# Attention's q products as 64-row halves of the array in token pairs, and inverse roots on VectorE

## The chip, the core and the metric

The kernel runs on one core of a Trainium2 chip. The metric is device microseconds of one execution; the median of three runs of the kernel before is 1817.77 us (1817.72 to 1819.34). TensorE (PE) multiplies, with its weight loads (PEld) recorded apart; VectorE (DVE), ScalarE (ACT) and GpSimd (POOL) work element by element; SyncE (SP) issues most of the DMAs. Each engine works through its own list in order.

## The reference

```python
kv = np.einsum('bhsd,bhse->bhde', k, v)          # batch 8, heads 8, seq 576, head_dim 64
out = np.einsum('bhsd,bhde->bhse', q, kv)
rms = np.sqrt(np.mean(out * out, axis=-1, keepdims=True) + 1e-06)
attn = (out / rms * g_norm).astype(np.float32)
x = attn.transpose(0, 2, 1, 3).reshape(4608, 512)
# then twice, with its own weights: x = (act(x @ w_gate) * (x @ w_val)) @ w_out
# act: sigmoid the first time, silu the second; w_gate, w_val 512 x 1536, w_out 1536 x 512
```

All is float32. The attention is linear: for each head a 64 x 64 product of k and v, then q times it, then a norm over the head's 64 values.

## The kernel before, in words

The two feed-forward layers hold nearly all of the arithmetic. They are four phases of matmuls (`PH`); phase 0, the first 400 us or so, runs `gv_plain` (lines 638 to 646) and `part_plain` (806), the later ones `gv_win` (709) and `out_win` (841). Attention is not a stage of its own. A short prologue does batch 0's k-v product and the first four token tiles; everything else of it stands in a queue of steps, `att`, and is dropped between the feed-forward matmuls of phase 0 by `tick`, early enough for the block of 512 tokens that needs it (`AHEAD`).

A token tile is 128 tokens of a batch with all 8 heads. There are 36: nine per pair of batches, and the fifth of each nine (i == R) holds the last 64 tokens of both batches; we call it a rest tile. For each tile `tok_q` and `tok_a` bring q transposed into `qT` (128 partitions: two heads of 64, by four head pairs, by 128 tokens), `tok_b` multiplies it with k-v (207 or 209) and squares the result on ACT (212), `tok_r` sums the squares (DVE, 216) and takes the inverse root, `tok_n` scales the product (239) into `xn`, and `tok_c` transposes it and sends it to memory. `STAGES` sets by how many tiles each step follows the first.

In `tok_b` the k-v product of a head pair is a block-diagonal 128 x 128 matrix in `kvz`, with zeros off the diagonal that POOL writes once. So a tile is four matmuls over all 128 rows of the array, 128 tokens as weights and 128 moving columns. Its result fills one PSUM bank of the pool `ps_g`, which has four and serves the gate and value products (`gv`) too. Each float32 matmul shows in the trace as two weight loads and two matmul records. A rest tile writes its two batches to the two 64-column halves of the array.

The inverse root is ACT's table function in the first four tiles, after which one Newton step follows on DVE; in the other 32 tiles it is `pow` on POOL (222) with the Newton step on POOL (230 to 233). ACT loads the table of `Abs_reciprocal_sqrt` at the start (84), and another when the first sigmoid comes (645).

Weights of later phases are prepared by `stage`: a list of small steps that begins with the loads of raw weights (`l0`, `l1`, `l2`), then `nop` steps that give the DMA time, and then `o1` and so on, of which `o1` (375) is ACT's and waits for the raw weights to land. PE, DVE and SP are ordered by a scheduler in this stretch; ACT and POOL go as the code is written.

Of the kernel before, what the change touches and what calls it, by code (L numbers as in the profile page):

```python
# [9 lines left out]
F32 = mybir.dt.float32  # L10
F32R = mybir.dt.float32r
U32 = mybir.dt.uint32
AF = mybir.ActivationFunctionType
ALU = mybir.AluOpType
AX = mybir.AxisListType
# [5 lines left out]
def attention_two_ffn(ctx: ExitStack, tc: tile.TileContext, q, k, v, g_norm, weights, out):  # L21
# [8 lines left out]
    nc = tc.nc  # L30
    B, H, S, D = q.shape
# [3 lines left out]
    P = 128  # L35
    NB = 512
    NBLK = NT // NB
    TPB = NB // P
    KD = DM // P
    NP = H // 2  # L40
    R = 4
    KB = 1024
    SM = R * P
    SR = S - SM
    TP = 2 * S // P
# [3 lines left out]
    sm = ctx.enter_context(tc.tile_pool(name="sm", bufs=4))  # L49
    dr = ctx.enter_context(tc.tile_pool(name="dr", bufs=1, space=DRAM))  # L50
    ps_o = ctx.enter_context(tc.tile_pool(name="ps_o", bufs=4, space=PSUM))
    ps_g = ctx.enter_context(tc.tile_pool(name="ps_g", bufs=4, space=PSUM))
# [4 lines left out]
    at = at_ctx.enter_context(tc.tile_pool(name="at", bufs=1, side="right"))  # L57
# [15 lines left out]
    early = tc.manual_schedule(engines={ET.Activation, ET.Pool})  # L73
    early.__enter__()
    ident = at.tile([P, P], F32, name="ident")
    kvz = [at.tile([P, NP, 2, D], F32, name=f"kvz{i}") for i in range(2)]
    gcol = at.tile([P, 1], F32, name="gcol")
    mhalf = at.tile([P, H], F32, name="mhalf")
    grow = at.tile([P, D], F32, name="grow")
    make_identity(nc, ident)  # L80
    for t in kvz:
        nc.gpsimd.memset(t, 0.0)
    nc.vector.memset(mhalf, -0.5)
    nc.scalar.activation(sm.tile([P, H], F32, tag="y", name="y"), mhalf, AF.Abs_reciprocal_sqrt)


    MANUAL = (0, 4)
    TA = 11
    SQ = 32
    QB, XT = 4, 5 * TPB  # L90
    kvt, qt, kvps, kvbd, qT, xn, xd = {}, {}, {}, {}, {}, {}, {}
    xr = {}
    for j in range(NBLK):
        t = dr.tile([DM, NB], F32, name=f"xd{j}")
# [39 lines left out]
    def run_of(b, nm, r, hs=slice(0, H)):  # L134

        if (b, nm, r) not in kvt:
            tag, n = ("ta", TA) if b == 0 else (nm + "s", 2)
            kvt[b, nm, r] = at.tile([P, H, D], F32, tag=tag, bufs=n, name=f"{nm}s")
# [20 lines left out]
                nc.tensor.matmul(kvps[b][e * D:(e + 1) * D, hp, :D], lt, rt, start=(r == hp == 0), stop=(r == R and hp == NP - 1), skip_group_check=True)  # L159

    def kv_mask(b):
        ps, z = kvps.pop(b), kvz[b % 2]
        for e in range(2):
            es = slice(e * D, (e + 1) * D)
            if b < 1:
                nc.vector.tensor_copy(out=z[es, :, e], in_=ps[es, :, :D])
            else:
                nc.scalar.activation(z[es, :, e], ps[es, :, :D], AF.Copy)
        kvbd[b] = z.rearrange("p a e d -> p a (e d)")

    def tok_q(tau):
        bp, i = divmod(tau, TP)
        b = 2 * bp + (i > R)
        if b >= QB and i != R:
            n = P // SQ
            src = kvt[b, "q"][:, :, (i if i < R else i - R - 1) * n:][:, :, :n]
            qT[tau] = at.tile([P, NP, P], F32, tag="ta", bufs=TA, name="qT")
            nc.vector.transpose(qT[tau].rearrange("p a (j c) -> p a j c", c=SQ), src)
# [3 lines left out]
    def tok_a(tau):  # L182
# [4 lines left out]
        for hp in range(NP):  # L187
# [5 lines left out]
            nc.tensor.transpose(ps[:, hp, :], src, ident)  # L193
        qT[tau] = at.tile([P, NP, P], F32, tag="ta", bufs=TA, name="qT")
        nc.scalar.activation(qT[tau], ps, AF.Copy)

    sqt, ost = {}, {}

    def tok_b(tau):
        bp, i = divmod(tau, TP)  # L200
        t = qT.pop(tau)
        ps = ps_g.tile([P, NP, P], F32, tag="g", name="ops")
        for hp in range(NP):
            if i == R:
                for e in range(2):
                    es = slice(e * SR, (e + 1) * SR)
                    nc.tensor.matmul(ps[es, hp, :], t[:, hp, es], kvbd[2 * bp + e][:, hp, :], start=True, stop=True)
            else:
                nc.tensor.matmul(ps[:, hp, :], t[:, hp, :], kvbd[2 * bp + (i > R)][:, hp, :], start=True, stop=True)  # L209
        ost[tau] = ps.rearrange("p a (b d) -> p (a b) d", d=D)  # L210
        sqt[tau] = at.tile([P, H, D], F32, tag="ta", bufs=TA, name="sq")
        nc.scalar.activation(sqt[tau], ost[tau], AF.Square)

    def tok_r(tau):
        a = sm.tile([P, H], F32, tag="a", name="a")
        nc.vector.tensor_reduce(a, sqt.pop(tau), axis=AX.X, op=ALU.add)
        (nc.vector if tau < TPB else nc.gpsimd).tensor_scalar(a, a, 1.0 / D, 1e-6, op0=ALU.mult, op1=ALU.add)
        y = sm.tile([P, H], F32, tag="y", name="y")
        if tau < TPB:
            nc.scalar.activation(y, a, AF.Abs_reciprocal_sqrt)  # L220
        else:
            nc.gpsimd.tensor_tensor(out=y, in0=a, in1=mhalf, op=ALU.pow)
        u = sm.tile([P, H], F32, tag="u", name="u")
        if tau < TPB:
            nc.vector.scalar_tensor_tensor(out=u, in0=y, scalar=-0.5, in1=y, op0=ALU.mult, op1=ALU.mult)
            nc.vector.tensor_tensor(out=u, in0=u, in1=a, op=ALU.mult)
            nc.vector.scalar_tensor_tensor(out=y, in0=u, scalar=1.5, in1=y, op0=ALU.add, op1=ALU.mult)
            sqt[tau] = y
            return
        nc.gpsimd.tensor_tensor(out=u, in0=y, in1=y, op=ALU.mult)  # L230
        nc.gpsimd.tensor_tensor(out=u, in0=u, in1=a, op=ALU.mult)
        nc.gpsimd.tensor_scalar(u, u, -0.5, 1.5, op0=ALU.mult, op1=ALU.add)
        nc.gpsimd.tensor_tensor(out=y, in0=y, in1=u, op=ALU.mult)
        sqt[tau] = y

    def tok_n(tau):
        y = sqt.pop(tau)
        xn[tau] = at.tile([P, H, D], F32, tag="ta", bufs=TA, name="xn")
        nc.vector.tensor_tensor(out=xn[tau], in0=ost.pop(tau), in1=y.unsqueeze(2).to_broadcast([P, H, D]), op=ALU.mult)
        if tau >= XT:  # L240
            nc.gpsimd.tensor_tensor(out=xn[tau], in0=xn[tau], in1=grow.unsqueeze(1).to_broadcast([P, H, D]), op=ALU.mult)

    def tok_c(tau):
        if tau >= XT:
# [30 lines left out]
    def attention_steps():  # L275

        st = []
        nt = B * S // P
        STAGES = ((0, tok_q), (1, tok_a), (3, tok_b), (3, tok_r), (4, tok_n), (5, tok_c))

        def run(t0, t1):
            for t in range(t0, t1 + 5):
                bp, i = divmod(t, TP)
                b = 2 * bp + (i >= R)
                z = i - R * (b % 2)
                on = t < t1 and b + 1 < B
                kv = list(kv_of(b + 1)) if on and z == 2 + b % 2 else []
                qs = [lambda b=b, a=a: load_q(b + 1, a) for a in range(NP)] if kv and b + 1 >= QB else []
                if t < t1 and i == 1:
                    st.append((t, lambda bp=bp: load_qr(bp)))  # L290
                for lag, f in STAGES:
                    if t0 <= t - lag < t1:
                        st.append((t - lag, lambda t=t - lag, f=f: f(t)))
                    if lag == 3:
                        st.extend((t, f) for f in kv[:1])
                        del kv[:1]
                        if not kv:
                            st.extend((t, f) for f in qs[:1])
                            del qs[:1]
                    elif not kv:  # L300
                        st.extend((t, f) for f in qs[:1])
                        del qs[:1]
                st.extend((t, f) for f in qs)
                if on and z == 3 + b % 2:
                    if b + 1 < QB:
                        st.append((t, lambda b=b: load_q(b + 1)))
                    if b + 2 < B:
                        st.append((t, lambda b=b: load_kv(b + 2)))

        st.append((TPB, lambda: load_kv(2)))  # L310
        run(TPB, nt)
        return st


    PROLOGUE = "w9 K q0 q1 a0 a1 q2 q3 w1 kv b0 a2 lq qr r0 b1 a3 r1 n0 w6 b2 r2 c0 n1 b3 r3 c1 n2 w3 c2 n3 c3 k6 w6"


    PH = [(0, 0, 6, False), (0, 6, 6, True), (1, 0, 6, True), (1, 6, 6, True)]
# [104 lines left out]
    def stage(f, m):  # L423
# [7 lines left out]
        e = m % 2  # L431
        paired = phase_of[f, m][0] in WOUT
        d = wd[f, m] = dr.tile([P, E + (0 if paired and not e else E if paired else 2 * DM)], F32, name=f"wd{f}_{m}")
        z = {}
# [16 lines left out]
        l0, o0, s0 = rounded(f, m - e, e, buf)  # L451
        l1, o1, s1 = rounded(f, m - e + 1, e, buf)
        l2, o2, s2 = rounded(f, m, 2, buf)

        def new(k):
            z[k] = buf("s")
# [6 lines left out]
        q0 = lambda i: lambda: s0["u"][:, i * Q:(i + 1) * Q]  # L463
        q1 = lambda i: lambda: s1["u"][:, i * Q:(i + 1) * Q]
        S = lambda k, i: lambda: z[k][:, i * Q:(i + 1) * Q]
        th = [l0, l1, nop, nop] + o0 + o1
        th += [lambda: (new(0), sm_(0, 0, q1(0), q1(1), ALU.add)())]
        th += [sm_(0, 1, S(0, 0), q0(0), ALU.subtract)]
        th += [lambda: (new(1), sm_(1, 0, q0(0), q1(0), ALU.subtract)())]
# [14 lines left out]
        ]  # L484
        if paired:
            return th + (stage_pair(f, m, buf, store, fl, hi, lo) if e else [])
        return th + [l2, nop, nop, nop] + o2 + [
            lambda: hi(fl(s2, 0, 2), s2["u"]),
            lambda: lo(fl(s2, 2, 4), s2["u"], fl(s2, 0, 2)),
            nop,  # L490
# [132 lines left out]
    ht, ops, part, pd = {}, {}, {}, {}  # L623
# [522 lines left out]
    for ph, (f, m0, n, win) in enumerate(PH):  # L1146
# [4 lines left out]
        for at_, (j, ms) in enumerate(visits):  # L1151
# [6 lines left out]
            for i in ms:  # L1158
# [42 lines left out]
                if tail and tail[0] + 1 < len(PH) and tail[1] == NBLK - 1 and PH[tail[0]][3]:  # L1201
                    z = tail[2] - PH[tail[0]][1]
# [53 lines left out]
```

## Time and profile before

| what | value |
|---|---|
| median of the runs | 1817.77 us |
| profiled execution, its own time | 1813.71 us |
| its span, first to last instruction | 1811.9 us |
| PE busy | 1776.1 us, 98% |
| DVE, ACT, POOL busy | 1055.2, 661.7, 684.5 us |
| granted TensorE clock, mean | 0.996 |

The profiled execution took 1.8 us more than its span, before the first or after the last instruction. The sums below are made against this execution, and a difference found there is carried over to the median, which is 4.06 us higher. A busy PE is one with a matmul under way; the mean duration of a matmul record is from its start to its end in the array, and several overlap, so the pace is read from how far the starts lie apart, or from the chain of waits, which gives each piece the time until the next one began.

### The profile page before, as it was taken

How to read it: one execution, taken by the hardware profiler on the slowest of the kernel's cores; microseconds unless marked ns; L12 is line 12 of the kernel's file. 1: busy time of each engine (PE TensorE's matmuls, PEld its weight loads, DVE VectorE, ACT ScalarE, POOL GpSimd, SP SyncE). 2: the span in 40 equal slices, each digit the busy share in tenths (PEclk: the TensorE clock that was granted, in tenths of full speed). 3: DMA queues.
4: the chain of work that ended last, by engine and by line, in shares of the span. 5: the costliest groups of instructions: out<-in, count | busy, mean ns of one | idle time of the engine just before them, and what ended most of it. 6: DMA issues, size and time to landing. Idle time of an engine off the chain costs nothing.

```text
span 1811.9 us, 31885 instructions
## 1 busy us (share of the span) xinstructions
PE 1776.1 (98%) x12298; PEld 1625.4 (90%) x12298; DVE 1055.2 (58%) x1754; ACT 661.7 (37%) x1349; POOL 684.5 (38%) x748
## 2 busy tenths in 40 slices
PE   5899999999999999999999999999999999999999
PEld 4688887888889999999999999999999999999998
DVE  5866466554335666666666565555553555555555
ACT  3654233333233333333333443334342333333332
POOL 1654355431012442442433443344441344444444
PEclk8999999999999999999999999999999999999999
DMA  9968875557236542434339755555567634343432
GB/s 265 271 176 222 236 195 154 139 148 242 93 116 250 181 136 91 146 99 135 127 130 402 282 182 176 190 186 187 192 231 286 232 129 129 129 129 129 129 129 71
DMA packets 274824, 320.38 MB, mean 177 GB/s; under 512 B 95856, under 2 KB 193392, under 8 KB 271984
## 3 DMA queue, kind: packets, MB, share of 16 engines
q1 hardware_dynamic: 259504, 305.24, 52.1%
q10 hardware_dynamic: 15168, 13.11, 2.5%
q8 instruction: 96, 1.57, 0.4%
q14 instruction: 56, 0.46, 0.1%
HBM read 191.14 MB, written 127.14 MB: 176 GB/s over the span
## 4 chain that ended last, share of the span: by engine, by line
PE 93%; DMA 2%; DVE 2%; SPq 1%; ACT 1%; issue 1%; POOL 0%; DVEq 0%; ACTq 0%
PE gv L709 44%; PE o L820 16%; PE gv L638 15%; PE o L806 8%; PE o L841 7%; PE ops L209 1%; DMA raw<-in_moe_w_out_dram 1%; PE kvps L159 1%; DMA xl<-xd 0%; DMA vm<-in_v_dram 0%; PE xTp L256 0%; PE qTp L193 0%; DMA raw<-in_moe_w_gate_dram 0%; ACT u L375 0%; SPq L126 0%
## 5 line engine op out<-in xcount | busy, mean ns | idle before, releaser
L709 PE MATMUL gv<-x,wgv 128*128 128x256 f32 x4536 | 549.3, 282 | 0.0
L709 PEld LDWEIGHTS gv<-x,wgv 128*128 128x128 f32 x4536 | 545.5, 189 | 2.8 <-DVE v L329 0.2
L638 PE MATMUL gv<-x,wgv 128*128 128x512 f32 x1296 | 314.3, 394 | 5.3 <-ACT sg L645 3.7
L638 PEld LDWEIGHTS gv<-x,wgv 128*128 128x128 f32 x1296 | 240.3, 188 | 56.7 <-ACT sg L645 4.6
L709 PEld LDWEIGHTS gv<-arena,wgv 128*128 128x128 f32 x2268 | 273.7, 190 | 2.8 <-DVE v L329 0.4
L709 PE MATMUL gv<-arena,wgv 128*128 128x256 f32 x2268 | 274.6, 282 | 0.1
L329 DVE TENSOR_TENSOR u<-u,gv 128x512 f32<-128x512 f32 x162 | 110.9, 684 | 260.5 <-PE gv L709 256.0
L697 POOL TENSOR_TENSOR h<-v,h 128x512 fp32r<-128x512 f32 x54 | 75.0, 1388 | 243.7 <-ACT h L693 243.4
L806 PE MATMUL o<-h,wo 128*128 128x512 f32 x648 | 164.2, 397 | 0.0
L682 ACT ACTIVATE w<-v 128x256 f32<-128x256 f32 x81 | 34.0, 420 | 313.8 <-DVE v L329 306.5
L806 PEld LDWEIGHTS o<-h,wo 128*128 128x128 f32 x648 | 120.0, 188 | 27.1 <-issue 0.3
L697 POOL TENSOR_TENSOR h<-w,h 128x512 fp32r<-128x512 f32 x54 | 70.7, 1310 | 140.6 <-ACT h L693 137.7
L820 PE MATMUL o<-arena,h 128*128 128x512 f32 x432 | 103.6, 395 | 0.0
L820 PE MATMUL o<-h,arena 128*128 128x512 f32 x432 | 103.3, 394 | 0.0
L646 DVE TENSOR_TENSOR sg<-sg,gv 128x512 f32<-128x512 f32 x54 | 36.9, 684 | 109.1 <-PE gv L638 108.9
L820 PEld LDWEIGHTS o<-arena,h 128*128 128x128 f32 x432 | 79.9, 188 | 17.9
L820 PEld LDWEIGHTS o<-h,arena 128*128 128x128 f32 x432 | 80.1, 188 | 17.5
L753 POOL TENSOR_TENSOR he<-w,he 128x256 fp32r<-128x256 f32 x27 | 20.0, 740 | 186.1 <-ACT he L752 186.1
L379 DVE TENSOR_SCALAR u<-u 128x512 uint32<-128x512 uint32 x72 | 36.2, 503 | 79.9 <-ACT u L375 79.9
L682 ACT ACTIVATE v<-g 128x256 f32<-128x256 f32 x81 | 34.0, 420 | 132.9 <-DVE g L329 132.9
L841 PE MATMUL o<-arena,he 128*128 128x256 f32 x648 | 82.1, 281 | 0.0
L329 DVE TENSOR_TENSOR g<-u,gv 128x512 f32<-128x512 f32 x81 | 55.7, 687 | 44.4 <-PE gv L709 42.7
(143 smaller groups left out, 2630.7 us busy)
## 6 DMA issues: line engine op xcount, KB each, us to landing
wgv<-wd SPq DMA_DIRECT2D x18, 1792.0 KB, 10.3
x<-xc SPq DMA_DIRECT2D x126, 256.0 KB, 4.6
pl<-pd SPq DMA_DIRECT2D x80, 256.0 KB, 4.3
pd<-ye SPq DMA_DIRECT2D x72, 256.0 KB, 2.6
xc<-arena SPq DMA_DIRECT2D x70, 256.0 KB, 3.5
wd<-raw SPq DMA_DIRECT2D x63, 256.0 KB, 2.9
xc<-x SPq DMA_DIRECT2D x56, 256.0 KB, 3.8
raw<-in_moe_w_gate_dram SPq DMA_DIRECT2D x24, 512.0 KB, 4.7
```

Of the source, the lines that this page charges most:

```text
L159: nc.tensor.matmul(kvps[b][e * D:(e + 1) * D, hp, :D], lt, rt, start=(r == hp == 0), stop=(r == R and hp == NP - 1), skip_group_check=True)
L329: nc.vector.tensor_tensor(out=out, in0=a, in1=b, op=ALU.add)
L379: nc.vector.tensor_scalar(ub, ub, 3, None, op0=ALU.logical_shift_left)
L638: nc.tensor.matmul(ps, w[:, e, a, kk, :], x[b][:, kk, :], start=(n == 0), stop=(n == 3 * KD - 1))
L646: nc.vector.tensor_tensor(out=sg, in0=sg, in1=bank[1], op=ALU.mult)
L682: nc.scalar.activation(o, t[:, 0], AF.Silu if f else AF.Sigmoid)
L697: nc.gpsimd.tensor_tensor(out=t[:, 1], in0=v, in1=t[:, 0].bitcast(F32), op=ALU.subtract)
L709: nc.tensor.matmul(ps[:, e], w[:, l, kk], xs[r // 5][:, r % 5, kk], start=(fresh and e == n == kk == 0), stop=(not more and e == 1 and n = ...
L753: nc.gpsimd.tensor_tensor(out=hs[z][:, 1], in0=x, in1=hs[z][:, 0].bitcast(F32), op=ALU.subtract)
L806: nc.tensor.matmul(ps, l, r, start=(fresh and t == 0), stop=(last and t == 2))
L820: nc.tensor.matmul(ps, l, r, start=(fresh and e == t == 0), stop=(last and e == 1 and t == 2))
L841: nc.tensor.matmul(ps[:, t], h[:, r, cs], w[:, Ax[a] + 7 * l], start=(start and t == n_ == 0), stop=(stop and t == 1 and n_ == 2), skip_gr ...
```

## The change

`kvz` holds the 64 x 64 products without zeros, 64 rows for each head of a pair, in three buffers. `tok_b` is called once for two tiles: each head is a matmul of its own over 64 rows of the array, with 128 tokens as weights and 64 moving columns; the even head of a pair uses the lower rows and writes one bank, the odd head the upper rows and another bank. Squares, sums and scaling go by bank, two calls for the two tiles. The inverse root is, for all tiles, ten operations on DVE over 128 x 16: a guess by integer arithmetic on the bits, and two steps that refine it. ACT's first table is that of the sigmoid. `xn` has two buffers of its own and the shared tag `ta` eight instead of eleven. The stages' order, the prologue's order and the number of `nop` steps in `stage` differ.

```diff
-    for t in kvz:
-        nc.gpsimd.memset(t, 0.0)
-    nc.scalar.activation(sm.tile([P, H], F32, tag="y", name="y"), mhalf, AF.Abs_reciprocal_sqrt)
+    nc.scalar.activation(sm.tile([P, H], F32, tag="s0", bufs=1, name="s0"), mhalf, AF.Sigmoid)
...
-    def tok_b(tau):
-        bp, i = divmod(tau, TP)
-        t = qT.pop(tau)
-        ps = ps_g.tile([P, NP, P], F32, tag="g", name="ops")
-        for hp in range(NP):
...
-                nc.tensor.matmul(ps[:, hp, :], t[:, hp, :], kvbd[2 * bp + (i > R)][:, hp, :], start=True, stop=True)
+    def tok_b(t1):
+        pss = [ps_g.tile([P, 2 * NP, D], F32, tag="g", name="ops") for _ in range(2)]
+        for k in range(2):
+            bp, i = divmod(t1 - 1 + k, TP)
+            t = qT.pop(t1 - 1 + k)
+            for hp in range(NP):
                 for e in range(2):
+                    es, to = slice(e * D, (e + 1) * D), pss[e][:, k * NP + hp]
+                    if i == R:
+                        for y in range(2):
+                            ys = slice(y * SR, (y + 1) * SR)
+                            nc.tensor.matmul(to[ys], t[es, hp, ys], kvbd[2 * bp + y][es, hp, :], start=True, stop=True)
+                    else:
+                        nc.tensor.matmul(to, t[es, hp, :], kvbd[2 * bp + (i > R)][es, hp, :], start=True, stop=True)
...
-            nc.gpsimd.tensor_tensor(out=y, in0=a, in1=mhalf, op=ALU.pow)
...
+        for k in range(2):
+            v.tensor_reduce(a[:, k], sqt[t1][k], axis=AX.X, op=ALU.add)
+        v.tensor_scalar(a, a, 1e-6, None, op0=ALU.add)
+        v.tensor_scalar(y.bitcast(U32), a.bitcast(U32), -0.5, float(0x5F3759DF), op0=ALU.mult, op1=ALU.add)
+        v.tensor_tensor(out=u, in0=y, in1=y, op=ALU.mult)
...
+        v.scalar_tensor_tensor(out=y, in0=u, scalar=1.5, in1=y, op0=ALU.add, op1=ALU.mult)
...
-        STAGES = ((0, tok_q), (1, tok_a), (3, tok_b), (3, tok_r), (4, tok_n), (5, tok_c))
+        STAGES = ((3, 1, tok_n), (0, None, tok_q), (1, None, tok_a), (2, 1, tok_b), (2, 1, tok_r), (4, 1, tok_c), (5, 0, tok_c))
...
-    PROLOGUE = "w9 K q0 q1 a0 a1 q2 q3 w1 kv b0 a2 lq qr r0 b1 a3 r1 n0 w6 b2 r2 c0 n1 b3 r3 c1 n2 w3 c2 n3 c3 k6 w6"
+    PROLOGUE = "w9 K q0 q1 a0 a1 q2 q3 w1 kv b1 a2 lq qr r1 a3 n1 w6 b3 c0 r3 c1 w3 n3 c2 c3 k6 w6"
...
-        th = [l0, l1, nop, nop] + o0 + o1
+        th = [l0, l1] + [nop] * 6 + o0 + o1
...
-        return th + [l2, nop, nop, nop] + o2 + [
+        return th + [l2] + [nop] * 6 + o2 + [
```

PE's list before, at a single tile in the second half of the attention (`ops` is the product of q, `gv` and `o` are the feed-forward's):

```order
L193 MATMUL qTp<-ident,qs 128x128 x4
L638 MATMUL gv<-x_311,wgv_3_999 128x512
L638 MATMUL gv<-x_310,wgv_3_999 128x512 x2
L638 MATMUL gv<-x_311,wgv_3_999 128x512
L209 MATMUL ops<-kvz_85,qT 128x128 x4
L638 MATMUL gv<-x_310,wgv_3_999 128x512 x2
```

And PE's list of the changed kernel at a pair:

```order
L804 MATMUL o<-h,wo_2_916 128x512 x9
L189 MATMUL qTp<-ident,qs 128x128 x4
L804 MATMUL o<-h,wo_2_916 128x512 x3
L208 MATMUL ops<-kvz_84,qT 128x64 x16
L636 MATMUL gv<-x_321,wgv_4_1271 128x512
L636 MATMUL gv<-x_322,wgv_4_1271 128x512
```

Two visits of four matmuls, 128 columns each, have become one visit of sixteen with 64 columns; two of the sixteen visits after the prologue are cut in two by other matmuls.

ACT's list before, at the first sigmoid (`raw` are weights as loaded, `wgv` weights in use):

```order
L143 ACTIVATE qs<-qm 128x512
L415 ACTIVATE wgv_1_490<-u 128x512
L645 ACT_TABLE_LOAD
L645 ACTIVATE sg<-gv 128x512
L195 ACTIVATE qT<-qTp 128x512
```

The same place in the changed kernel:

```order
L191 ACTIVATE qT<-qTp 128x512
L413 ACTIVATE wgv_1_495<-u 128x512
L643 ACTIVATE sg<-gv 128x512
L141 ACTIVATE qs<-qm 128x512
L373 ACTIVATE u<-raw 128x512
```

The table load in front of the sigmoid is gone, and no other stands in its place.

DVE's list of the changed kernel, at the first inverse roots after the prologue (`u<-raw`, `s<-u`, `s<-raw` prepare weights; the rows of 128x16 are the root's):

```order
L218 TENSOR_REDUCE a<-sq 128x8 x2
L381 SCALAR_TENSOR_TENSOR u<-raw,u 128x512
L219 TENSOR_SCALAR a<-a 128x16
L385 TENSOR_SCALAR s<-u 128x512
L220 TENSOR_SCALAR y<-a 128x16
L388 SCALAR_TENSOR_TENSOR s<-raw,s 128x512
L221 TENSOR_TENSOR u<-y 128x16
L327 TENSOR_TENSOR u<-u,s 128x512
L222 TENSOR_TENSOR u<-u,a 128x16
L377 TENSOR_SCALAR u<-u 128x512
L223 TENSOR_SCALAR w<-u 128x16
```

Before, none of the small rows stood in this list after the prologue; now each is followed by a long one.

## Rows read from the trace of the kernel before

**Rows 1.** The page, busy time of each engine, with share and count.
```profile
PE 1776.1 (98%) x12298; PEld 1625.4 (90%) x12298; DVE 1055.2 (58%) x1754; ACT 661.7 (37%) x1349; POOL 684.5 (38%) x748
```

**Rows 2.** Windows: length, PE, PEld, DVE, ACT, POOL busy, clock, DMA share, GB/s.
```profile
0.00:39.65 39.65, 19.38 (x225) 17.20 (x225) 19.06 (x44) 13.87 (x26) 5.74 (x11) 0.87 0.96 259
39.65:100.00 60.35, 53.02 (x429) 44.19 (x426) 47.92 (x77) 40.07 (x73) 35.16 (x51) 0.97 1.01 280
100.00:400.00 300.00, 296.28 (x1713) 245.01 (x1712) 175.34 (x282) 111.83 (x201) 138.88 (x203) 1.00 0.66 176
```

**Rows 3.** Waits of PE from 39 to 400 us: total us, times, longest.
```profile
PE gv L638 <- ACT sg L645: 3.7, 2, 3.5
PE ops L207 <- ACT sg L645: 1.8, 1, 1.8
PE qTp L193 <- ACT qs L143: 1.4, 1, 1.4
PE ops L209 <- DVE xn L239: 1.2, 1, 1.2
...
PE gv L638 <- POOL y L222: 0.7, 1, 0.7
```

**Rows 4.** The chain of waits between 90 and 200 us: start, us, what.
```profile
97.79 0.89 PE ops L209 x8
...
111.98 1.02 PE ops L207 x16
113.01 2.07 PE gv L638 x8
115.08 2.63 PE kvps L159 x80
...
187.11 1.83 PE gv L638 x8
```

**Rows 5.** Windows for line 638 after a pause: PE, PEld busy (started), clock.
```profile
62.76:62.86 0.10, 0.07 (x1) 0.10 (x1) 1.00 0.95 317
62.76:62.88 0.12, 0.09 (x1) 0.12 (x2) 1.00 1.04 350
```

**Rows 6.** The same for line 207, 64-column weights, after a pause.
```profile
50.12:50.16 0.04, 0.03 (x2) 0.03 (x2) 1.00 1.51 563
50.12:50.19 0.07, 0.06 (x2) 0.06 (x4) 1.00 1.15 424
```

**Rows 7.** The same for line 193, transposes, after a pause.
```profile
66.77:66.82 0.05, 0.04 (x1) 0.04 (x1) 1.00 1.24 230
66.77:66.85 0.08, 0.07 (x1) 0.07 (x2) 1.00 1.17 221
```

**Rows 8.** Timeline of ACT at the first sigmoid: start, us, instruction.
```profile
48.18 1.28 ACT L645 ACT_TABLE_LOAD   x1
49.48 0.60 ACT L645 ACTIVATE sg<-gv 128x512 f32<-128x512 f32 x1
```

**Rows 9.** The chain of waits at PE's longest pause after the prologue.
```profile
272.26 4.76 DMA raw<-in_moe_w_gate_dram
...
277.13 0.66 ACT u L375
277.79 0.49 ACT sg L645
...
278.32 5.74 PE gv L638 x24
```

**Rows 10.** Timeline of DVE in and after the prologue.
```profile
17.49 0.86 DVE L166 COPY kvz<-kvps 64x256 f32<-64x256 f32 x2 [7.84 <-PE kvps L159]
...
24.06 0.17 DVE L225 SCALAR_TENSOR_TENSOR u<-y 128x8 f32<-128x8 f32 x1 [0.28 <-ACT y L220]
24.26 0.17 DVE L226 TENSOR_TENSOR u<-u,a 128x8 f32<-128x8 f32 x1
...
41.31 0.43 DVE L379 TENSOR_SCALAR u<-u 128x512 uint32<-128x512 uint32 x1 [2.54 <-ACT u L375]
...
46.53 1.48 DVE L379 TENSOR_SCALAR u<-u 128x512 uint32<-128x512 uint32 x1
```

**Rows 11.** Groups by line and shape: count, busy us, mean ns, idle before.
```profile
L222 POOL TENSOR_TENSOR y<-a,mhalf 128x8 f32<-128x8 f32 x32 | 55.4, 1731 | 2.7
```

More of the change, by code (lines that the diff above doesn't have):

```diff
@@ L75, in attention_two_ffn @@
     ident = at.tile([P, P], F32, name="ident")
-    kvz = [at.tile([P, NP, 2, D], F32, name=f"kvz{i}") for i in range(2)]
+    kvz = [at.tile([P, NP, D], F32, name=f"kvz{i}") for i in range(3)]
     gcol = at.tile([P, 1], F32, name="gcol")
@@ L80, in attention_two_ffn @@
     make_identity(nc, ident)
-    for t in kvz:
-        nc.gpsimd.memset(t, 0.0)
     nc.vector.memset(mhalf, -0.5)
-    nc.scalar.activation(sm.tile([P, H], F32, tag="y", name="y"), mhalf, AF.Abs_reciprocal_sqrt)
+    nc.scalar.activation(sm.tile([P, H], F32, tag="s0", bufs=1, name="s0"), mhalf, AF.Sigmoid)
     MANUAL = (0, 4)
-    TA = 11
+    TA = 8
     SQ = 32
@@ L161, in kv_mask @@
     def kv_mask(b):
[L162 to L169, printed above, removed]
+        ps, z = kvps.pop(b), kvz[b % 3]
+        if b < 1:
+            nc.vector.tensor_copy(out=z, in_=ps[:, :, :D])
+        else:
+            nc.scalar.activation(z, ps[:, :, :D], AF.Copy)
+        kvbd[b] = z
     def tok_q(tau):
@@ L197, in attention_two_ffn @@
     sqt, ost = {}, {}
-    def tok_b(tau):
-        bp, i = divmod(tau, TP)
-        t = qT.pop(tau)
-        ps = ps_g.tile([P, NP, P], F32, tag="g", name="ops")
-        for hp in range(NP):
-            if i == R:
-                for e in range(2):
-                    es = slice(e * SR, (e + 1) * SR)
-                    nc.tensor.matmul(ps[es, hp, :], t[:, hp, es], kvbd[2 * bp + e][:, hp, :], start=True, stop=True)
-            else:
-                nc.tensor.matmul(ps[:, hp, :], t[:, hp, :], kvbd[2 * bp + (i > R)][:, hp, :], start=True, stop=True)
-        ost[tau] = ps.rearrange("p a (b d) -> p (a b) d", d=D)
-        sqt[tau] = at.tile([P, H, D], F32, tag="ta", bufs=TA, name="sq")
-        nc.scalar.activation(sqt[tau], ost[tau], AF.Square)
@@ L214, in tok_r @@
[L214 to L221, printed above, removed]
-            nc.gpsimd.tensor_tensor(out=y, in0=a, in1=mhalf, op=ALU.pow)
[L223 to L241, printed above, removed]
+    def tok_b(t1):
[4 more added lines that the diff above has]
+            for hp in range(NP):
+                for e in range(2):
+                    es, to = slice(e * D, (e + 1) * D), pss[e][:, k * NP + hp]
[3 more added lines that the diff above has]
+                            nc.tensor.matmul(to[ys], t[es, hp, ys], kvbd[2 * bp + y][es, hp, :], start=True, stop=True)
+                    else:
+                        nc.tensor.matmul(to, t[es, hp, :], kvbd[2 * bp + (i > R)][es, hp, :], start=True, stop=True)
+        ost[t1] = pss
+        sqt[t1] = [at.tile([P, 2 * NP, D], F32, tag="ta", bufs=TA, name="sq") for _ in range(2)]
+        for e in range(2):
+            nc.scalar.activation(sqt[t1][e], pss[e], AF.Square, scale=D**-0.5)
@@ new lines, in tok_r @@
+    def tok_r(t1):
+        v = nc.vector
+        a, y, u, w = [sm.tile([P, 2, 2 * NP], F32, tag=n, bufs=2, name=n) for n in "ayuw"]
+        for k in range(2):
[3 more added lines that the diff above has]
+        v.tensor_tensor(out=u, in0=y, in1=y, op=ALU.mult)
+        v.tensor_tensor(out=u, in0=u, in1=a, op=ALU.mult)
+        v.tensor_scalar(w, u, 0.375, -1.25, op0=ALU.mult, op1=ALU.add)
+        v.tensor_tensor(out=w, in0=w, in1=u, op=ALU.mult)
+        v.scalar_tensor_tensor(out=y, in0=w, scalar=1.875, in1=y, op0=ALU.add, op1=ALU.mult)
+        v.scalar_tensor_tensor(out=u, in0=y, scalar=-0.5, in1=y, op0=ALU.mult, op1=ALU.mult)
+        v.tensor_tensor(out=u, in0=u, in1=a, op=ALU.mult)
+        v.scalar_tensor_tensor(out=y, in0=u, scalar=1.5, in1=y, op0=ALU.add, op1=ALU.mult)
+        sqt[t1] = y
@@ new lines, in tok_n @@
+    def tok_n(t1):
+        y, pss = sqt.pop(t1), ost.pop(t1)
+        x = at.tile([P, 2 * NP, 2, D], F32, tag="xn", bufs=2, name="xn")
+        for e in range(2):
+            nc.vector.tensor_tensor(out=x[:, :, e], in0=pss[e], in1=y[:, e].unsqueeze(2).to_broadcast([P, 2 * NP, D]), op=ALU.mult)
+        for k in range(2):
+            t = xn[t1 - 1 + k] = x[:, k * NP:(k + 1) * NP].rearrange("p a b d -> p (a b) d")
+            if t1 - 1 + k >= XT:
+                nc.gpsimd.tensor_tensor(out=t, in0=t, in1=grow.unsqueeze(1).to_broadcast([P, H, D]), op=ALU.mult)
@@ L290, in run @@
                     st.append((t, lambda bp=bp: load_qr(bp)))
-                for lag, f in STAGES:
-                    if t0 <= t - lag < t1:
+                for lag, odd, f in STAGES:
+                    if t0 <= t - lag < t1 and odd in (None, (t - lag) % 2):
                         st.append((t - lag, lambda t=t - lag, f=f: f(t)))
-                    if lag == 3:
+                    if f in (tok_b, tok_r):
                         st.extend((t, f) for f in kv[:1])
```

## The prediction

> **What bounds the kernel now.** I read the busy times of the engines first. PE is busy for 98% of the span and DVE for 58% [rows 1], so time is saved where PE has less to do or waits less, and lost where it waits more. The windows then tell where the change can act. All attention work lies in the first 400 us. Up to 39.65 us, the prologue, PE is busy for 19.4 us only; from 39.65 to 100 it is idle for 60.35 - 53.02 = 7.3 us; from 100 to 400 for 3.7 us [rows 2]. The granted clock is 0.97 and 1.00 in the last two stretches, so nearly all of it runs at the upper of the two levels, 2.4 GHz. The reader is to see two things in these windows: after 100 us nothing counts but PE's own work and one odd pause, and before 100 us DVE is nearly as full as PE, with 47.9 of 60.35 us.
>
> The waits of PE name what it waited for between 39 and 400 us [rows 3]. The longest, 3.5 us, ends with an ACT sigmoid, and the chain of waits shows why that one was late: ACT's list had come to a weight step that waited for raw weights, issued at 272.26 and landed 4.76 us later, and the sigmoid stood behind it [rows 9]. The second, 1.8 us, also ends with a sigmoid, in front of which ACT spent 1.28 us on a table load [rows 8].
>
> **The q products on PE.** A single tile now takes 0.89 us of PE in the chain, eight records, so one per 0.11 us; a rest tile takes 1.02 us, and the eight gv records behind it 2.07 us where eight of them elsewhere take 1.83 us [rows 4]. That last difference, 0.24 us, is the price of leaving the shape with 64 columns; on entering, 1.02 less sixteen records at two per 0.11 us (0.89) leaves 0.13 us. So one visit in another shape of the array costs 0.37 us beside its work. Line 207 also shows that two halves do work at once: sixteen records of 128 moving columns need the time of eight.
>
> In the change, a pair of tiles has sixteen matmuls, 32 records, of 64 moving columns. No trace of before has a weight load of 64 rows and 128 columns, so its pace is bounded by the nearest rows. The k-v products have 64 moving columns and 64-column weights in two halves; their 80 records take 2.63 us, less the 0.13 us of entry 0.0625 us for each two [rows 4]. That is the fast end. But there a weight load has 64 columns, and the second two loads begin between 0.04 and 0.07 us after the first two, say 0.05 [rows 6]; at line 638, with 128 weight columns, the second load begins only 0.10 to 0.12 us after the first, say 0.11, though nothing but the first load stands in its way, since the first matmul has hardly begun [rows 5]. Before, a load of 0.11 us hides behind a matmul of 0.11 us. After, the matmul of 64 columns is half as long, the tokens are still 128 weight columns, and the load is what sets the pace. I take 0.11 us for each two records, with both row halves loading side by side as the two column halves do at line 207. A pair without a rest tile is then 16 x 0.11 + 0.37 = 2.13 us, against 2 x 0.89 = 1.78 now: 0.35 us more. Twelve such pairs after the prologue: +4.2 us.
>
> The rule that speaks against this change is in the Trainium skill, "TensorE: Matmul & The Clock Gate", section "LDWEIGHTS (loading the stationary operand)": the time of a weight load goes by its columns, not by its rows, and is columns divided by 1.2 in ns, 107 ns for 128. The 0.10 to 0.12 us of the row on line 638 agree for 128 rows; no run so far shows 64 rows. By its figure the sum would be as above.
>
> Four pairs hold a rest tile. Now: 0.89 + 1.02 + 0.24 = 2.15 us. After: the plain tile 8 x 0.11 = 0.88; the rest tile has 32 records in four quarters of the array with 64-column loads, between 8 x 0.0625 = 0.50 us (four at once) and 16 x 0.0625 = 0.99 us (two at once); the visit 0.37, and the change of shape within it, half of a visit's price, 0.19. Together 1.94 to 2.43 us, so -0.2 to +0.3 each; I take the middle, +0.1 us for the four. Two of the sixteen visits are cut in two by other matmuls: 2 x 0.37 = +0.7 us. PE's work in all: 4.2 + 0.1 + 0.7 = +5.0 us.
>
> **What PE waits for less.** The table load goes from its place before the first sigmoid to the start, where ACT is idle: -1.3 us, of the 1.8 us that PE waited there [rows 3, 8]. The 0.7 us wait for POOL's root [rows 3] goes, since POOL has no roots any more; it spent 55.4 us in `pow` alone, 1.73 us each [rows 11]. The nop steps between the raw weights' load and ACT's first step on them go from two and three to six. That puts ACT's waiting step behind the sigmoid on which PE stood for 3.5 us [rows 9], so -3.5 us; the other end is nothing, if a late load meets another sigmoid. In the prologue the k-v copy is one of 0.43 us instead of two in 0.86 [rows 10]: -0.4 us; pairs start later there and the roots need no ACT, and I let these cancel. Together -5.9 us.
>
> **What DVE has more.** A small operation takes 0.17 us and the next one begins 0.20 us after it [rows 10], so ten are 2.0 us for each pair. Past 100 us that is 24 us for twelve pairs in a stretch where DVE is busy for 175 of 300 us, and I count it at nothing: it lies in 125 us of DVE idle time, and costs PE up to 24 us if that cover were gone. From 39.65 to 100 us it is 8.0 us for four pairs on an engine with 12.4 us left [rows 2]. DVE's list is in order: behind a small row stand weight steps, the gate product that frees a gv bank, and `xn`, which frees both banks of the pair; behind these PE has the next transposes or gv matmuls in its list. Two of the four gv banks are now held together, where before one was. The bounds are -1.1 us and +8.0 us: below, because the same weight step took 1.48 us at 46.53 and 0.43 us at 41.31 [rows 10] with POOL at work beside it, and POOL has less; above, because none of it may fit. I take the middle, +3.5 us. The waits for `xn` that PE has now, 1.2 us [rows 3], stay in this.
>
> **The sum.** 5.0 - 5.9 + 3.5 = +2.6 us, on the profiled execution 1813.71 to 1816.3 us. That execution lies 4.06 us below the median of the runs; the same +2.6 us on the median gives **1820.4 us**, no change within what can be told (0.2%, 3.6 us).
>
> **Rivals.** *The loads keep up (B).* If a 64-row load of 128 columns takes no longer than the matmul, the pace is that of the k-v products, 0.0625 us for two records. For it speaks that transposes, with weights of the same 128 columns, begin their second load within 0.08 us [rows 7], so the array can take them faster; against it, that every other row with 128 columns has 0.11. A pair is then 16 x 0.0625 + 0.37 = 1.37 us, -0.41 us, twelve of them -4.9; a pair with a rest tile 0.50 + 0.50 + 0.56 = 1.56, -0.59, four of them -2.4; with the two cuts -6.6 us. With -5.9 + 3.5 us of waits: -9.0, 1808.8 us. The Trainium skill's "TensorEngine Tiling (Array Packing)", section "Theoretical Speedup", promises up to twice the speed for a contraction of 64 or less; this rival is what it would make here, and no row of before has row halves to bear it out.
>
> *The halves load one after the other (C).* The change doesn't do what it says. Then 32 x 0.11 + 0.37 = 3.89 us for a pair, +2.11, twelve of them +25.3; with a rest tile 1.76 + 32 x 0.05 + 0.56 = 3.92, +1.77, four of them +7.1; cuts +0.7. With -2.4 us of waits: +30.7, 1848.5 us. Line 207, where two loads start within 0.04 us [rows 6], speaks against it; but these are column halves.
>
> *DVE becomes the bound (D), slower than before.* PE as forecast, but all 8.0 us of the roots before 100 us end up in PE's waits: 5.0 - 5.9 + 8.0 = +7.1, 1824.9 us. It decides from where less than about half of the 8.0 us finds room in DVE's idle time. For it speaks DVE's 79% there; against it, the 12.4 us left and that each small row follows a long one, so that none waits for the one before it.
>
> **How the numbers follow.** I give the forecast 0.45, B 0.30, C 0.08 and D 0.17. The forecast's own range is 1815 to 1829: PE +4 to +6, waits -5.9 or -2.4, DVE -1.1 to +8. Of its 0.45, 0.27 lie within 0.2%, 0.15 above and 0.03 below. B is faster but for 0.01, C slower, D slower but for 0.02. So faster 0.03 + 0.29 = 0.32, same 0.27 + 0.01 + 0.02 = 0.30, slower 0.15 + 0.08 + 0.15 = 0.38. The range, 1806 to 1831, holds the forecast, D and most of B, and leaves C out.
>
> **What would show it.** In the profile after: the pace of the `ops` records and of their weight loads, 0.11 us for two (forecast, D), 0.06 (B) or 0.22 (C); a pair in the chain at about 2.1 us with the gv piece behind it; no table load at the first sigmoid; no PE wait of 3 us behind a raw load; PE's idle time from 40 to 100 us at about 7.3 - 2.0 + 3.5 = 8.8 us and from 100 to 400 under 1 us. The prediction is wrong if the pace of loads is another than at line 638, if late raw loads meet other sigmoids, or if PE waits for `xn` at many pairs.

## The result and the profile after

| kernel | median us (runs) | ratio to before, 95% interval |
|---|---|---|
| before, measured beside it | 1817.77 (5) | |
| after | 1833.69 (5; 1828.21 to 1838.62) | 1.0080 [1.0054, 1.0105] |

The change makes the kernel 15.9 us slower, where 2.6 us were forecast; the time lies above the range. The page's busy times, columns as in [rows 1]:

```profile
PE 1788.7 (98%) x12618; PEld 1631.1 (89%) x12618; DVE 1100.5 (60%) x1917; ACT 653.2 (36%) x1337; POOL 590.7 (32%) x554
```

PE has 12.6 us more and DVE 45 more, POOL 94 less. The profiled execution, here the median one, spans 1831.9 us, 20.0 more than before's. To see where, I counted the feed-forward matmuls (gv and o records, 11178 in each kernel, in the same order but for less than 100 places) and took the start of the one with the same number in each trace. Lengths in us, from the start of one such matmul to that of another:

| stretch, by before's time | before | after | early_raw | quarters_both |
|---|---|---|---|---|
| prologue, 0 to 39.6 | 39.6 | 44.1 | 38.3 | 38.9 |
| 39.6 to 122 | 82.7 | 84.7 | 85.2 | 81.1 |
| 122 to 292 | 169.8 | 180.5 | 172.3 | 165.5 |
| 292 to 391 | 98.7 | 100.6 | 102.4 | 98.8 |
| 391 to 856 | 464.8 | 465.1 | 465.1 | 464.5 |
| 856 to 1014 | 158.3 | 163.3 | 163.6 | 158.4 |
| 1014 to 1430 | 416.5 | 416.0 | 416.1 | 416.0 |
| 1430 to 1786 | 355.8 | 351.8 | 351.8 | 351.8 |

(The last two columns are experiments of the next section.) After loses 4.5 us in the prologue, 2.0 and 10.7 in the next two stretches, 1.9 up to 391, 5.0 near 1000, and gains 4.0 in the last. One k-v product (80 records, 2.63 us at the upper clock level) lies in the second stretch in before and in the third in the three others, so by equal work after loses 4.6 and 8.1 us in these two.

PE's waits after, from 39 to 400 us, as in [rows 3]:

```profile
PE kvps L157 <- ACT sg L643: 6.0, 2, 5.4
PE qTp L189 <- DVE xn L235: 2.1, 1, 2.1
PE qTp L189 <- ACT qs L141: 2.0, 2, 1.4
PE ops L206 <- DVE sg L644: 1.6, 1, 1.6
```

The 3.5 us behind a sigmoid and POOL's 0.7 us are gone, but the first row is a new wait of 5.4 us, longer than any in [rows 3]. The windows, columns as in [rows 2], with the same 60.35 us after the first gv matmul:

```profile
44.14:104.49 60.35, 53.56 (x463) 44.23 (x459) 52.54 (x103) 33.23 (x61) 12.62 (x9) 0.89 0.87 248
100.00:400.00 300.00, 292.76 (x1914) 239.05 (x1913) 196.21 (x399) 108.89 (x197) 54.97 (x46) 0.99 0.67 179
```

Idle time in the first is 6.8 us, less than before's 7.3, though the granted clock is 0.89 in place of 0.97; in the second it is 7.2 us and not under 1. The chain of waits tells what the 5.4 us were (start, us, what), and the windows around it what followed:

```profile
208.10 0.45 PE xTp L254 x4
...
208.57 0.70 ACT xT L256
...
209.29 0.37 ACTq L263
...
209.70 0.60 ACTq L576
...
210.37 6.10 DMA xl<-xd
...
216.53 0.32 SPq L438
...
218.60 5.74 DMA raw<-in_moe_w_out_dram
...
224.36 0.66 ACT u L373
225.02 0.50 ACT sg L643
...
225.56 4.73 PE kvps L157 x80
```

```profile
215.00:223.35 8.35, 5.05 (x60) 3.65 (x56) 2.42 (x4) 0.00 (x0) 0.00 (x0) 1.00 1.03 339
223.35:230.18 6.83, 4.62 (x80) 4.43 (x80) 4.99 (x9) 3.38 (x6) 0.00 (x0) 0.50 0.84 238
```

Read from the bottom: PE needs the sigmoid, which stands in ACT's list behind a weight step that waits for a raw load. SP issued that load only at 218.60, because in its list it stands behind wd stores (L438), and these waited until an xl load of ACT's had landed; that one was issued behind the xd store of a transposed tile. When PE went on, the clock was at 0.50, the lower level, and the 80 k-v records took 4.73 us where they took 2.63 [rows 4]. The same chain stands in the trace of before:

```profile
197.11 6.10 DMA xl<-xd
...
203.23 4.86 DMA raw<-in_moe_w_out_dram
...
208.11 0.67 ACT u L375
208.78 0.50 ACT sg L645
```

There PE waited 0.26 us for it. In after the xl load is issued 13.3 us later, while the last feed-forward matmul ahead of the pause starts only 11.1 us later (219.75 against 208.66), so the xl load is 2.2 us late against PE's work; four wd stores (2.1 us), which in before were issued while that transfer still ran, now stand between its landing and the raw load; and the raw transfer takes 0.9 us more. The three make 5.2 us, by which this pause is longer than before's 0.26.

The q products themselves run as forecast. Part of the chain, and windows of line 208 alone (length, PE busy and records, PEld busy and loads started, clock):

```profile
103.94 1.93 PE ops L208 x32
105.87 2.30 PE o L804 x9
...
117.63 1.04 PE ops L208 x16
118.67 0.62 PE ops L206 x32
```

```profile
103.96:104.00 0.04, 0.04 (x2) 0.04 (x4) 1.00 1.19 384
103.96:104.10 0.14, 0.14 (x4) 0.14 (x6) 1.00 1.13 373
103.96:104.21 0.25, 0.25 (x6) 0.25 (x8) 1.00 1.11 365
```

Two records more in each 0.105 us: both halves load side by side. The nine o records behind a pair take 2.30 us where they take 2.10 without a change of shape (fullrows, below), so a pair costs 2.13 us.

### The profile page after: what moved, and what is told of

The parts are those of the page before. It is cut to its first block, busy times and chain, and to the rows that moved or that the text cites. A ratio compares the mean times of both kernels' runs of the same rounds, so it can differ in the third digit from the quotient of the medians.

```text
span 1831.9 us, 32485 instructions
## 1 busy us (share of the span) xinstructions
PE 1788.7 (98%) x12618; PEld 1631.1 (89%) x12618; DVE 1100.5 (60%) x1917; ACT 653.2 (36%) x1337; POOL 590.7 (32%) x554
## 4 chain that ended last, share of the span: by engine, by line
PE 90%; DMA 4%; DVE 3%; ACT 1%; issue 1%; SPq 1%; POOL 0%; ACTq 0%; DVEq 0%; POOLq 0%
PE gv L707 41%; PE o L818 15%; PE gv L636 15%; PE o L804 8%; PE o L839 7%; PE ops L208 2%; DMA xc<-arena 1%; DMA raw<-in_moe_w_out_dram 1%; PE kvps L157 1%; DMA xl<-xd 1%; PE xTp L254 1%; DMA vm<-in_v_dram 1%; PE qTp L189 0%; DVE u L327 0%; DMA wd<-s 0%
## 5 line engine op out<-in xcount | busy, mean ns | idle before, releaser
L458 POOL TENSOR_TENSOR s<-u 128x256 f32<-128x256 f32 x36 | 31.4, 872 | 188.1 <-DVE u L327 137.2
L327 DVE TENSOR_TENSOR v<-g,gv 128x512 f32<-128x512 f32 x81 | 55.5, 685 | 40.4 <-PE gv L707 39.9
L691 ACT ACTIVATE h<-w 128x512 fp32r<-128x512 f32 x54 | 34.1, 632 | 127.5 <-PE o L818 89.7
```

The source lines that it names most:

```text
L327: nc.vector.tensor_tensor(out=out, in0=a, in1=b, op=ALU.add)
L458: nc.gpsimd.tensor_tensor(out=z[k][:, i * Q:(i + 1) * Q], in0=x(), in1=y(), op=op)
L691: nc.scalar.activation(t[:, 0], v, AF.Copy)
```

## The experiments

Theory 1 after the result was that the order of DMAs, not PE or DVE, makes most of the miss; rivals were the halves, the roots on DVE, the empty steps. All medians are of four runs or more, against before run beside them (1816.54 us in the first four, 1817.27 in the next, 1817.82 in the last). "Less than the change" is a difference of medians; by the ratios it is 1 to 2 us smaller. The interval of the change's own ratio is 4.6 us to either side, so by the runs alone the differences of oldnops and later_x, 3.5 and 4.6 us, are not clear of noise, and that of fullrows hardly is; these rest on the traces.

**fullrows**: the paired order with the old block-diagonal products, and other numbers of buffers to make room (the line of the product, shortened).

```diff
-                    nc.tensor.matmul(to, t[es, hp, :], kvbd[...][es, hp, :], ...)
+                nc.tensor.matmul(ps[:, hp, :], t[:, hp, :], kvbd[...][:, hp, :], ...)
```

> The changed kernel with block-diagonal products over all 128 rows again, in pairs (two k-v buffers and seven instead of eight buffers of the shared tag, for room); roots, stages and nop steps as changed. Theory 1 (the row halves cost what their weight loads cost, 2.13 us a pair against 1.78, and twice that at the half clock in the prologue; the rest is pauses that don't hang on the halves): 5 us less in PE's work and 2 to 3 us less in the prologue, so about 1826 us, the pause of PE near 225 us still there. Rival (the halves cause the pauses too, since pairs in halves hold the banks longer): back to 1815 to 1820 us, without the pause.

1827.35 us, 1.0052 [1.0038, 1.0065]. The halves cost 6.3 us of the 15.9; the pause stays, 5.3 us at 220.

```profile
100.68 1.78 PE ops L210 x16
102.46 2.10 PE o L807 x9
```

**quarters**: each product of a half cut again into two of 64 tokens, 64 x 64 each.

```diff
-                        nc.tensor.matmul(to, t[es, hp, :], kvbd[...][es, hp, :], ...)
+                        for y in range(2):
+                            ys = slice(y * D, (y + 1) * D)
+                            nc.tensor.matmul(to[ys], t[es, hp, ys], kvbd[...][es, hp, :], ...)
```

> The changed kernel with every tile in four quarters of the array, as its rest tiles are: weights of 64 columns, 64 moving columns. Theory 1 (the pace of a visit is that of its weight loads, which go by columns): four records per 0.06 us instead of two per 0.105, a pair 16 x 0.06 + 0.37 = 1.3 us against 2.13; 12 pairs 10 us and 4 pairs with a rest tile 2.4 us less, some 3 us less in the prologue: about 1818 us if the pauses stay. Rival (only records count, or the shape's cost): twice the records, so 1833 us or more.

1818.60 us, 1.0006 [0.9997, 1.0014], 15.1 us less than the change. Twice the records take 1.09 us, against 1.93 as halves and 1.78 as full rows:

```profile
97.15 1.09 PE ops L210 x64
```

The pause stays here too, 6.4 us at 214. The halves had 0.92 times the speed of full rows (1.78 / 1.93), the quarters, with half the weight columns in each load, 1.6 times (1.78 / 1.09). By the Trainium skill, "TensorEngine Tiling (Array Packing)", section "Theoretical Speedup", a dimension of 64 or less can give up to twice the speed; both measured values lie under that bound.

**oldnops**: the change with the old two and three empty steps behind raw loads.

```diff
-        th = [l0, l1] + [nop] * 6 + o0 + o1
+        th = [l0, l1, nop, nop] + o0 + o1
-        return th + [l2] + [nop] * 6 + o2 + [
+        return th + [l2, nop, nop, nop] + o2 + [
```

> The changed kernel with the former two and three nop steps in the staging of weights. Theory 1 (the pause near 225 us is raw weights issued late by SP behind stores and q loads, the nop steps too few to matter or in the wrong place): the pause stays, and the one near 278 us of the kernel before comes back: 1833 to 1838 us. Rival (the six nop steps made the pause, by moving loads behind other transfers): without it about 1823 us.

1830.22 us, 1.0067 [1.0054, 1.0080]: 3.5 us less than the change, below theory 1's range and above the rival's. The pause at 225 stays (5.6 us), so the empty steps did not make it; the waits near 1020 are gone:

```profile
PE gv L707 <- ACT u L714: 2.5, 1, 2.5
PE gv L707 <- DVE v L327: 1.8, 1, 1.8
```

These two rows are after's waits from 1000 to 1100 us; oldnops has none there. Its stretch from 856 to 1014 is 4.9 us shorter than after's, but the one from 122 to 292 is 2.8 us longer.

**poolroots**: the roots of the pairs after the prologue by `pow` on POOL again (`g` is POOL, `mh` holds -0.5).

```diff
+        if t1 >= TPB:
...
+            g.tensor_tensor(out=y, in0=a, in1=mh, op=ALU.pow)
...
+            return
```

> The changed kernel with the inverse roots of all pairs after the prologue on POOL, by pow and one Newton step over 128 x 16, as the kernel before has them per tile. Theory 1 (DVE's 32 us more cost little): 1830 to 1836 us, with PE's waits for xn about as long. Rival (DVE's list is what holds PE: banks come free late, and steps move): at least 8 us less, 1825 us or below, and no PE wait for xn between 60 and 100 us.

1856.75 us, 1.0215 [1.0200, 1.0229]. PE now waits 18 us for scaled products:

```profile
PE gv L646 <- DVE xn L245: 10.6, 5, 3.9
PE xTp L264 <- DVE xn L245: 7.5, 2, 3.9
```

This is 23 us slower than the change and outside both expectations: with tiles in pairs POOL is the worse place for the roots. What DVE's roots cost by themselves it does not show. The pause is here as well (5.5 us), so it belongs to what these four kernels share: the order in pairs and of the stages.

**later_x**: the change, with the xl loads four steps later in their queue; **before_later_x**, the same edit on before.

```diff
-            return L[:3] + [nop] * 6 + [S[0], L[3], nop, S[1], nop, S[2], nop, nop, S[3]]
+            return [nop] * 4 + L[:3] + [nop] * 6 + [S[0], L[3], nop, S[1], nop, S[2], nop, nop, S[3]]
```

> The change, with the loads of a block's x (xl<-xd, issued by ACT) put four steps later in their queue; nothing else. Theory 1 (DMA order): PE's 5.4 us pause at 225 us is an ACT u step waiting for a raw load that SP could issue only after four wd stores, which stood behind ACT's xl loads, which stood behind PE's transposes. With the xl loads issued after the raw load that pause goes, and with it the 6.9 us at the lower clock: about 9 to 11 us less than the change, 1823 to 1825 us. Theory 2 (DVE or the halves themselves make sg late at that place): the pause stays, time 1833 us as the change. Under both the 1020-us pause stays.

> Control: the kernel before with the same four steps ahead of the xl loads. It has no pause at that place (0.26 us), so theory 1 expects no change of more than 2 us from 1817 us, with the 3.5 us pause at 278 us still there or moved by other reasons. If it is faster by 5 us or more, the later loads help by something else than the pause of the paired order, and the run of the change with them says nothing about it.

later_x 1829.11 us, 1.0060 [1.0048, 1.0073], 4.6 less than the change where 9 to 11 were expected; before_later_x 1818.52 us, 1.0002 [0.9993, 1.0011], as expected. (Its trace has the pause near 278, here of 4.2 us, and behind it the clock at 0.50 for 6.83 us; in before's trace the clock stays up there.) The pause is halved: one xl load was still ahead of the stores.

```profile
209.91 4.62 DMA xl<-xd
...
216.42 4.72 DMA raw<-in_moe_w_out_dram
...
222.36 3.66 PE kvps L157 x73
```

The raw load goes out 2.2 us earlier and lands a microsecond faster; PE waits 2.7 us.

**early_raw**: the change, with the raw load itself moved ahead of six wd stores; **before_early_raw**, the same on before.

```diff
             lambda: (store(0, fl(s0, 0, 2)), store(7 * Q, fl(s0, 2, 4))),
+            *([] if paired else [l2]),
...
-        return th + [l2] + [nop] * 6 + o2 + [
+        return th + [nop] * 6 + o2 + [
```

> The change, with the raw load of an output slab issued nine steps earlier in the weight queue, ahead of six of the eight wd stores that stood before it in SP's list; the step that reads it stays where it was. Theory 1 (DMA order): later_x took away half of the pause at 225 us because the stores still stood behind xd and one xl transfer; with the raw load ahead of them ACT's u step finds its data, the whole pause of 5.4 us goes, and with it the time at the lower clock: 9 to 11 us less than the change, 1823 to 1825 us. Theory 2 (the raw buffer is freed too late, or the transfer itself is slow then): the raw load is still late, 1829 to 1834 us.

> Control: the kernel before with the same move of the raw load. Its 3.5 us pause at 278 us is behind such a raw load, so theory 1 expects it to go or to shrink: 1813 to 1815 us. Theory 2: 1817 us, nothing moves.

early_raw 1823.32 us, 1.0032 [1.0020, 1.0044], 10.4 less than the change; before_early_raw 1812.63 us, 0.9974 [0.9964, 0.9984]. SP's and ACT's lists in early_raw (start, us, instruction):

```profile
206.81 0.33 SPq L366 DMA_DIRECT2D raw<-in_moe_w_out_dram  x1
...
211.12 1.45 SPq L438 DMA_DIRECT2D wd<-raw  x3
```

```profile
213.00 0.66 ACT L373 ACTIVATE u<-raw 128x512 f32<-128x512 f32 x1 [7.09 <-DMA raw<-in_moe_w_out_dram]
213.56 0.58 ACT L644 ACTIVATE sg<-gv 128x512 f32<-128x512 f32 x1
```

The stores still stand until 211, but the raw load no longer behind them, and PE's longest wait for a sigmoid from 39 to 400 us is 0.3 us. In the profiled executions the stretch from 122 to 292 is 8.2 us shorter than after's and the next one 1.8 longer; the prologue is 5.9 shorter, which this edit does not explain (see below). The gain on before was expected at 3 to 5 us and measured at 5.2, but its trace keeps 2.7 of the 3.5 us pause at 278, so I can't say where it came from.

**before_newnops**: the kernel before with six empty steps (the edit of oldnops turned round).

> The kernel before with the change's six empty steps behind the raw loads. Theory 1 (the empty steps act alike in both kernels): the pause of 3.5 us at 278 us goes, as predicted, and a pause of some 4 to 5 us near 1000 to 1020 us comes; in all 1817 to 1820 us. Theory 2 (the pause near 1020 belongs to the paired order): 3.5 us less, 1813 to 1814 us.

1817.34 us, 1.0004 [0.9995, 1.0013]. The pause at 278 goes; one of 1.4 us at 311 and 3.0 us of waits near 1000 (2.3 and 0.7) come:

```profile
PE gv L709 <- ACT u L716: 2.3, 1, 2.3
PE gv L638 <- ACT sg L645: 2.1, 2, 1.4
...
PE gv L709 <- DVE v L329: 1.1, 2, 0.7
```

The stretch from 856 to 1014 us takes 163.0 us here, 163.3 to 164.4 in the six paired kernels with six empty steps, and 158.0 to 158.4 in the seven kernels, paired or not, with two and three. So the empty steps cost 5 us there whatever the tiles are.

**quarters_later_x, quarters_early_raw, quarters_both**: quarters and the old empty steps, with the later xl loads, the early raw load, or both.

> The change with 64x64 quarters for all tiles, the old two and three empty steps behind the raw loads, and the xl loads four steps later. Theory 1 adds what each showed alone: quarters 1818.6 us, the old empty steps -3.4, the pause at 214 us and its slow clock -9: about 1806 us, faster than both kernels. Theory 2 (the pauses only move to the next raw load): 1812 to 1819 us.

> The change with 64x64 quarters, the old empty steps and the early raw load, the xl loads where the change has them. Theory 1: no pause at 209 to 214 us, so at most the 1804 us of the kernel with later xl loads, which kept 2.6 us of it; about 1799 to 1804 us. Theory 2: the pause is back, 1812 to 1816 us.

> The same with the xl loads four steps later as well. Theory 1: the remaining pause of 2.6 us of quarters_later_x goes, with some 2 us at the lower clock: 1799 to 1802 us. Theory 2: 1804 us, as quarters_later_x.

1804.08 us, 0.9926 [0.9914, 0.9939]; 1803.71, 0.9922 [0.9910, 0.9935]; 1801.37, 0.9911 [0.9898, 0.9924]. All three came close to theory 1 and beat both kernels, the last by 16 us against before. The longest waits of PE in it from 39 to 400 us:

```profile
PE qTp L189 <- DVE xn L237: 2.8, 1, 2.8
PE qTp L189 <- ACT qs L141: 2.0, 2, 1.3
```

## Why the prediction was wrong

**The q products, +5.0 us: right.** Two records per 0.105 us, a pair 2.13 us, both as forecast; a pair with a rest tile 1.04 + 0.62 us and 0.2 on leaving, a little below the 1.94 to 2.43. Rivals B (0.0625) and C (0.22) fall at the upper clock level. The rows of before were the right ones to size it by [rows 4, 5]. By the Trainium skill, "TensorE: Matmul & The Clock Gate", section "LDWEIGHTS (loading the stationary operand)", a load's columns set its time and its rows do not; the 0.105 us for loads of 64 rows and 128 columns agree. The halves' 6.3 us against fullrows hold this term and the next.

**The same products at the lower level, and the prologue, -0.4 us: missing.** I priced pairs at 2.4 GHz alone. Where the clock is granted at 0.50 one takes 3.61 us, as this window of early_raw over one pair shows, behind a wait for xn:

```profile
67.19:70.80 3.61, 3.61 (x33) 3.49 (x34) 2.29 (x4) 0.39 (x1) 0.00 (x0) 0.50 1.18 214
```

The prologue has two pairs. In after they took 3.61 and 4.12 us, in early_raw, with the same instructions, 2.05 and 2.30:

```profile
21.16 3.61 PE ops L208 x32
...
26.67 4.12 PE ops L208 x28
```

```profile
19.13 2.05 PE ops L208 x32
...
22.79 2.30 PE ops L208 x28
```

That is 3.4 of the 5.9 us between these two prologues. After's is 4.5 us longer than before's, early_raw's 1.3 shorter, where I had forecast -0.4 and let the rest cancel. The records of after's clock don't show a lower level at that time, so here it is inferred from the durations (oldnops and later_x have the long ones too, poolroots the short ones); executions differ in it, and what decides it is open.

**What PE waits for less, -5.9 us: this step failed.** Its largest part, -3.5, said that six empty steps put ACT's waiting step behind the sigmoid, and named as its other end "nothing, if a late load meets another sigmoid". At 278 us [rows 9] it did what I said, and in before_newnops too, where the stretch from 122 to 292 is 3.3 us shorter. But the end of a wait that moves is not nothing: a late load met another sigmoid at 225 us, for 5.4 us, with 6.8 us at the lower level, in which the k-v records took 2.1 us more. I had looked at the nop steps and never at what delays the load: it is issued by SP behind stores that wait for transfers of another queue, and the order in pairs made these 2.2 us late and put the stores behind them. early_raw takes the load out of that line: the pause goes, and the time falls by 10.4 us (8.7 by the ratios). The empty steps then cost 5.0 us near 1000, which I had put at nothing (oldnops gains 3.5 net; before_newnops comes out even). The 1.3 us for the table load [rows 8] came to 0.2: the load is gone, but PE waits 1.6 us at that place for a gate product, which was late next. Only POOL's 0.7 came as forecast.

**The roots on DVE, +3.5 us: about right in size, and not idle time.** PE's idle time in the 60.35 us fell to 6.8 us, where 8.8 were forecast. But idle time is not the whole price. At the first pair after the prologue each root row stands behind a weight step, so that the ten take from 63.36 to 70.87; PE waits 2.1 us for xn, and then the clock is granted at 0.50 for 6.83 us (first and last root row, the window, and the chain):

```profile
63.36 0.16 DVE L219 TENSOR_SCALAR a<-a 128x16 f32<-128x16 f32 x1
...
70.70 0.17 DVE L228 SCALAR_TENSOR_TENSOR y<-u,y 128x16 f32<-128x16 f32 x1
```

```profile
73.17:80.00 6.83, 6.83 (x41) 6.03 (x39) 5.34 (x11) 4.24 (x8) 1.28 (x1) 0.50 1.12 306
```

```profile
72.61 3.07 PE ops L208 x32
75.68 1.05 PE xTp L254 x4
...
78.43 2.87 PE o L804 x9
```

From 72.61 to 81.30 PE does a pair, eight transposes and eleven o records in 8.7 us; at the upper level they take 1.93, 0.88 and 2.6 us, so 3.3 us are lost (an estimate from these rows). With the 0.9 us by which the wait for xn is longer than before's 1.2 [rows 3], that is about 4 us. The traces of all ten kernels in pairs have such a stretch of the lower clock near 70 us, and none of the four with single tiles has. What of it hangs on the roots being on DVE and what on the pairs was not run apart. Rival D's 8.0 us of waits did not come; poolroots, with POOL's 1.73 us for each tile of before [rows 11], shows that POOL would have been worse.

**The sum.** The forecast missed by 13.3 us of the median, and by 17.4 between the two profiled executions (20.0 against 2.6), where alone the parts can be read. They are 7.5 for the late raw load (5.4 waited, 2.1 on the k-v records), 5.0 for the empty steps near 1000, 4.9 for the prologue in executions like the profiled one, 1.1 for the table load, less 4.0 gained in the last stretch, which no step had. That makes 14.5; the other 2.9 are small pieces that I have not taken apart.

## What to carry to other kernels

Before a wait is counted as gone, follow the load behind it back to its issue: a DMA that stands in one engine's list behind stores that wait for another queue's transfers is late by all of them, and a reordering far away moves them. Issue such a load as soon as its buffer is free, not when its reader is due, as early_raw does. When a matmul is cut by rows, cut its weights' columns too, or the loads keep their pace (here two halves per 0.105 us, four quarters per 0.07); and price each visit, and each wait ahead of it, at both levels of the clock.

## What the runs showed that I had not expected

Products of 64 x 64 run four at once, 64 records in 1.09 us, 0.07 us for four; halves of 64 x 128 two at once, in 0.105 us. At the lower level the halves' pace fell to 3.61 / 16 = 0.23 us for two.

From 1430 to 1786 us, where PE never waits and its weight loads are never idle, the same matmuls take 355.84 us in all four kernels with single tiles and 351.84 in all ten with pairs, to 0.01 us: 118.6 ns against 117.3 from one record to the next. Attention is long over there; what the pairs change for it, perhaps the places of the buffers, was not tried and stays open.
